# Next batch's query and key steps as single instructions, and 14 weight conversion turns moved to earlier batches

## The chip, the cores and the metric

The kernel runs on one core of a Trainium2 chip. The metric is the time of one execution on the device, in microseconds (us). The engines are named as in the profile: PE (TensorE, matrix products), DVE (VectorE), ACT (ScalarE), POOL (GpSimd), SP (SyncE, which issues all transfers here). Each works through its own instructions in its own order and waits on semaphores for the others.

## The reference

```
# attention over 8 batches, 8 heads, 576 positions, head size 64
q_s = exp(q - max over a head of q);  q_s /= sum over the head + 1e-9
k_s = exp(k - max over positions);    k_s /= sum over positions + 1e-9
x   = q_s @ (k_s^T @ v)                        # 576 x 512 per batch
# gated MLP
h = gelu_tanh(x @ w_in);  u, v = halves of h
v_n = layer_norm(v) * g_ln
x   = x + (u * (w_sg @ v_n + b_sg)) @ w_out
# mixing over positions and over channels
u = x + (x^T @ U @ V)^T
out = u + relu(u @ w_ch1) @ w_ch2              # 512 -> 2048 -> 512
```

## The kernel before

Every product is made of three PE passes over operands split in a high part (`xh`, rounded) and a low part (`xl`, the rest). So behind most results ACT copies the high part, and DVE or POOL subtracts it to get the low part.

Eight batches run one after the other, numbered 0 to 7, each in the same stages. The V stage (`emit_Vh`, five row tiles t = 0 to 4) gives the v half of h in `pv`; ACT applies the gelu to give `ge`, DVE takes mean and variance (`stats`), and `emit_ln` normalizes. The V stage also transposes the batch before (`emit_yT`, tiles `pt`, `yh`, `yl`) and does its small mixing product (`pp`, `pst`, `pw`, `yt`), which goes to DRAM as `u2d`. The U stage (`emit_Uh`, four blocks f) gives the u half in `pu`, whose gelu is `ut`. The S stage (`emit_S`) mixes positions in `pS`, and DVE makes `gt`, `gl` from it. The y stage multiplies by w_out in `py` and adds x to give `yt`; the next batch's attention products stand around it. After batch 7 comes the long product with w_ch1 and w_ch2 (tile `mm`, recursive in the manner of Strassen, over stored weight combinations `wd` that are read back as `wu`), which PE does from about 632 us to the end.

During the stages of batch b the queries and keys of batch b + 1 are made ready on DVE, ACT and POOL, in five row tiles of 128 rows (the last holds 64 queries): `q_max` (tile `qm`), `q_sub`, `q_exp`, `q_sum` (tile `qs`), `q_total`, `q_norm`, `k_sub` and `k_exp`. The queries come into one tile `qt`, loaded by `load_q` in two transfers (rows of tiles 0 to 3, line 133, and the last 64 rows, line 134) during the y stage of the batch before.

The weights w_ch1 and w_ch2 arrive as float64 pairs of words and are converted piece by piece beside the batches. A turn (`turn`, a 'T' in the table `TURNS`) moves this by a step: load `stg` (SP), clamp it (L171, mostly POOL), shift its exponent (L177, ACT), merge the words (L183 and L184, DVE), add blocks to factors (`f<-f,f`, POOL or DVE), copy the high part to `chw` (ACT), subtract it (POOL or DVE), and store to `wd` (SP). `TURNS[b]` gives the turns after each V tile, U block, S block, y block; `STEP_TURNS` and `GROUP_TURNS` go on from there after batch 7, until all weights are done. In batch 7 the first tiles of the channel product (`us`, `uh`, `ul`) are made as well, by `u_first` and `u_parts`.

The order on PE is by hand. The order on DVE is the order of the code (`in_order(dve)`); on ACT, POOL and SP a scheduler sets it in the batches. An instruction that waits holds back what is behind it on its engine. On SP a transfer whose source isn't ready holds back the loads behind it.

Of the kernel before, what the change touches and what calls it, by code (L numbers as in the profile page):

```python
# [22 lines left out]
def fused_kernel(tc, q, k, v, w_in, g_ln, w_sgT, b_sg, w_out, U, V, w_ch1, w_ch2, outT):  # L23
# [412 lines left out]
    def k_exp(b, tiles=range(NT + 1)):
        kt = k_t[b]
        for t in tiles:
            act.activation(kt[:, t], kt[:, t], AF.Exp)
# [13 lines left out]
    def q_sub(b, t, eng=dve):
        n = TR[t]
        tt(eng, q3(t), q3(t), q_s[b][0:n, t].unsqueeze(2).to_broadcast([n, H, D]), ALU.subtract)

    def q_exp(b, t):
        act.activation(qt[0 : TR[t], t], qt[0 : TR[t], t], AF.Exp)

    def q_sum(b, t):  # L460
        if t == 0:
            q_s[b] = tmpp.tile([P, NT + 1, H], F32, tag="qs", name="qs")
        s = q_s[b]
        dve.tensor_reduce(out=s[0 : TR[t], t], in_=q3(t), op=ALU.add, axis=mybir.AxisListType.X)

    def q_total(b):

        s = q_s[b]
        for part in (s[:, 0:NT], s[0:R, NT]):
            dve.tensor_scalar(out=part, in0=part, scalar1=1e-9, scalar2=None, op0=ALU.add)  # L470
            dve.reciprocal(out=part, in_=part)
# [728 lines left out]
    with in_order(dve, act, pool, sp):  # L1200
# [13 lines left out]
        for t in (0, 1):  # L1214
            q_max(0, t)
            q_sub(0, t, dve if t in (3,) else pool)
            q_exp(0, t)
# [4 lines left out]
        k_spread(0)
        for t in range(NT + 1):
            k_sub(0, t)
            k_exp(0, (t,))
            if 0 < t < NT:
                q_exp(0, t + 1)
# [6 lines left out]
        q_total(0)
        for t in range(NT + 1):
            q_norm(0, t, dve)
            if t == 1:
# [16 lines left out]
    for b in range(B):  # L1254
# [52 lines left out]
        late_k = []  # L1307
        for f in range(NF):
# [8 lines left out]
            if f == 0:  # L1317
                emit_ln(b, NT)
                if nxt:
                    load_v(nxt)  # L1320
                else:
                    next(prep, None)
            if nxt:
                for t in Q_SUB[b > 0][f]:
                    q_sub(nxt, t, pool if t in Q_SUB_POOL[b > 0] else dve)
                for t in K_SUB[b > 0][f]:
                    if f >= spread_at:
                        k_sub(nxt, t)
                    else:
                        late_k.append(t)  # L1330
                if f == spread_at:
                    for t in late_k:
                        k_sub(nxt, t)
            if b > 0:
                slot(TURNS[b][1][f])
        if nxt:
            with contextlib.nullcontext() if b else tc.issue_after(last['g', 3].ins):
# [4 lines left out]
            for t in range(NT + 1):  # L1342
                q_sum(nxt, t)
            q_total(nxt)
            for t in range(NT + 1):
                q_norm(nxt, t, dve if t < Q_NORM_DVE[b > 0] else pool)
# [170 lines left out]
```

## Time and profile before

| what | value |
|---|---|
| median of 3 runs | 1308.29 us (1307.48 to 1314.53) |
| the profiled execution | 1311.05 us, span in the trace 1309.2 us |
| PE | busy 1260.0 us, 96% |
| weight loads of PE | busy 1139.1 us, 87% |
| DVE | busy 969.0 us, 74% |
| ACT | busy 636.9 us, 49% |
| POOL | busy 330.4 us, 25% |
| mean granted PE clock | 0.991 of full speed |

Times in the rows count from the start of the span. PE has 49 us of the span without work, and it runs at a lower clock for some stretches; the batches take the first 632 us.

### The profile page before, as it was taken

How to read it: one execution, taken by the hardware profiler on the slowest of the kernel's cores; microseconds unless marked ns; L12 is line 12 of the kernel's file. 1: busy time of each engine (PE TensorE's matmuls, PEld its weight loads, DVE VectorE, ACT ScalarE, POOL GpSimd, SP SyncE). 2: the span in 40 equal slices, each digit the busy share in tenths (PEclk: the TensorE clock that was granted, in tenths of full speed). 3: DMA queues.
4: the chain of work that ended last, by engine and by line, in shares of the span. 5: the costliest groups of instructions: out<-in, count | busy, mean ns of one | idle time of the engine just before them, and what ended most of it. 6: DMA issues, size and time to landing. Idle time of an engine off the chain costs nothing.

```text
span 1309.2 us, 20581 instructions
## 1 busy us (share of the span) xinstructions
PE 1260.0 (96%) x7592; PEld 1139.1 (87%) x7592; DVE 969.0 (74%) x1406; ACT 636.9 (49%) x979; POOL 330.4 (25%) x426
## 2 busy tenths in 40 slices
PE   4799999999999999898999999999999999999998
PEld 3598999999898989798888888888888889999998
DVE  7888879787988888788668953598337963694485
ACT  4756656575757466654454512444134422451342
POOL 4634152624243333665340202000010002000000
PEclk9899999999999999998999999999999999999999
DMA  8515171725343352468998667678756788899896
GB/s 268 164 47 171 37 218 37 225 70 167 96 151 120 111 168 73 162 208 299 312 344 315 227 231 257 209 242 290 257 193 226 243 285 297 269 304 315 260 290 215
DMA packets 135907, 274.14 MB, mean 209 GB/s; under 512 B 15232, under 2 KB 56704, under 8 KB 135808
## 3 DMA queue, kind: packets, MB, share of 16 engines
q1 hardware_dynamic: 135808, 272.84, 63.2%
q8 instruction: 60, 0.98, 0.3%
q14 instruction: 39, 0.32, 0.1%
HBM read 224.56 MB, written 48.23 MB: 208 GB/s over the span
## 4 chain that ended last, share of the span: by engine, by line
PE 79%; DVE 7%; DMA 4%; ACT 2%; issue 1%; POOL 1%; SPq 0%; DVEq 0%; ACTq 0%; POOLq 0%
PE mm L52 50%; PE pS L52 6%; PE pu L52 6%; PE pv L52 5%; PE py L52 5%; DMA stg<-in_w_ch_dram 1%; PE pm L52 1%; PE pp L52 1%; PE px L52 1%; PE pt L698 1%; DVE yt L55 1%; DVE f L183 1%; PE pk L52 1%; PE pt L527 1%; DMA wu<-wd 1%
## 5 line engine op out<-in xcount | busy, mean ns | idle before, releaser
L52 PE MATMUL mm<-oh,wu 128*128 128x512 f32 (+1 forms) x1120 | 320.7, 367 | 0.0
L52 PE MATMUL mm<-uh,wu 128*128 128x512 f32 (+1 forms) x1064 | 303.7, 366 | 1.9 <-DMA wu<-wd 1.1
L52 PEld LDWEIGHTS mm<-oh,wu 128*128 128x128 f32 x1120 | 207.0, 188 | 26.1
L52 PEld LDWEIGHTS mm<-uh,wu 128*128 128x128 f32 x1064 | 196.3, 188 | 26.4 <-issue 1.4
L52 PE MATMUL mm<-ol,wu 128*128 128x512 f32 (+1 forms) x560 | 205.7, 367 | 0.0
L61 ACT ACTIVATE oh<-h 128x1024 fp32r<-128x1024 f32 (+1 forms) x140 | 135.2, 973 | 124.8 <-PE mm L52 102.4
L52 PE MATMUL mm<-ul,wu 128*128 128x512 f32 (+1 forms) x532 | 194.9, 366 | 0.0
L55 DVE TENSOR_TENSOR ol<-h,oh 128x1024 fp32r<-128x1024 f32 (+1 forms) x140 | 155.4, 1113 | 40.9 <-ACT oh L61 40.1
L55 POOL TENSOR_TENSOR ust<-ust 128x1024 f32<-128x1024 f32 (+1 forms) x16 | 36.4, 2282 | 389.4 <-DMA ust<-u2d 348.8
L55 DVE TENSOR_TENSOR h<-mm,u 128x1024 f32<-128x1024 f32 (+1 forms) x57 | 63.3, 1111 | 87.8 <-PE mm L52 87.7
L52 PEld LDWEIGHTS mm<-ol,wu 128*128 128x128 f32 x560 | 105.2, 188 | 13.1
L55 DVE TENSOR_TENSOR u<-mm,u 128x1024 f32<-128x1024 f32 (+1 forms) x53 | 58.9, 1111 | 76.7 <-PE mm L52 71.3
L52 PEld LDWEIGHTS mm<-ul,wu 128*128 128x128 f32 x532 | 99.9, 188 | 12.1
L55 POOL TENSOR_TENSOR chw<-f,chw 128x256 fp32r<-128x256 f32 x98 | 78.9, 820 | 95.4 <-ACT chw L61 95.3
L55 DVE TENSOR_TENSOR h<-h,h 128x1024 f32<-128x1024 f32 (+1 forms) x80 | 88.9, 1112 | 0.0
L1041 ACT ACTIVATE h<-mm 128x1024 f32<-128x1024 f32 (+1 forms) x19 | 17.8, 938 | 130.8 <-PE mm L52 130.8
L1032 ACT ACTIVATE h<-h 128x1024 f32<-128x1024 f32 (+1 forms) x60 | 58.1, 969 | 33.9 <-DVE h L55 33.9
L61 ACT ACTIVATE chw<-f 128x256 fp32r<-128x256 f32 x112 | 42.6, 412 | 62.7 <-DVE f L184 23.1
L61 ACT ACTIVATE u<-mm 128x1024 f32<-128x1024 f32 (+1 forms) x24 | 22.5, 939 | 103.1 <-PE mm L52 86.9
L171 POOL TENSOR_SCALAR stg<-stg 128x256 f32<-128x256 f32 (+1 forms) x83 | 41.0, 496 | 99.7 <-DMA stg<-in_w_ch_dram 39.0
L52 PE MATMUL py<-gh,wo_h 128*128 128x288 f32 x256 | 57.6, 307 | 3.0 <-DVE gt L665 2.1
L52 PE MATMUL py<-gl,wo_h 128*128 128x288 f32 x256 | 56.0, 301 | 3.4 <-DVE gl L55 3.4
(165 smaller groups left out, 2650.2 us busy)
## 6 DMA issues: line engine op xcount, KB each, us to landing
wu<-wd SPq DMA_DIRECT2D x280, 512.0 KB, 4.4
wd<-chw SPq DMA_DIRECT2D x112, 256.0 KB, 3.6
stg<-in_w_ch_dram SPq DMA_DIRECT2D x64, 256.0 KB, 3.7
u2d<-yt SPq DMA_DIRECT2D x32, 288.0 KB, 2.4
vt<-in_v_dram SPq DMA_DIRECT2D x32, 256.0 KB, 6.7
qt<-in_q_dram SPq DMA_DIRECT2D x7, 1024.0 KB, 8.1
kt<-in_k_dram SPq DMA_DIRECT2D x7, 1024.0 KB, 6.1
res<-u2d SPq DMA_DIRECT2D x12, 512.0 KB, 5.3
```

The costliest lines, as they stand in the source:

```text
L52: pe.matmul(out, lhsT, rhs, start=first, stop=last, skip_group_check=onto)
L55: return eng.tensor_tensor(out=out, in0=a, in1=b, op=op)
L61: return act.activation(out, src, AF.Copy)
L171: eng.tensor_scalar(out=hi, in0=hi, scalar1=F64_MOST, scalar2=-F64_MOST, op0=ALU.min, op1=ALU.max)
L183: dve.tensor_scalar(out=b, in0=b, scalar1=3, scalar2=None, op0=ALU.logical_shift_left)
L527: pe.transpose(pt[:, t * P : (t + 1) * P], qt[:, t, c * P : (c + 1) * P], ident)
L698: pe.transpose(pt[0:n, c * P : (c + 1) * P], y_t[b][:, c, t * P : t * P + n], ident)
L1032: act.activation(h, h, AF.Relu)
L1041: act.activation(h_out(j, 11, n), bank, AF.Relu)
```

## The change

The query and key steps of the next batch become one instruction each over all five tiles, where there were five: `q_max`, `q_sub`, `k_sub`, `q_exp`, `k_exp`, `q_sum`, and `q_norm` (in two pieces for the batch after batch 0); `q_total` treats the whole tile in one pair of instructions. The whole `q_max` stands at V tile 0 (at tile 1 in batch 0), the whole `q_sub` at U block 1, the whole `k_sub` at U block 3. The first batch's own preparation stays in tiles. `emit_ln` of the last tile moves from behind U block 0 to behind block 1. The small instruction that makes `sh` becomes a tensor_scalar with two scalars in place of a scalar_tensor_tensor with two tensors. Two of the buffers of `u_parts` change places. `TURNS` of batches 2 to 5 gains 3, 4, 4 and 4 turns, that of batch 7 loses 4 in the V stage, 1 in the U stage and 5 in the S stage; 5 fewer are left for the stretch behind the batches.

```diff
-    def k_sub(b, t, eng=dve):
-        kt = k_t[b]
-        tt(eng, kt[:, t], kt[:, t], kx_t[b], ALU.subtract)
+    ALL = slice(0, NT + 1)
+
+    def k_sub(b, ts=ALL):
+        k = k_t[b][:, ts]
+        tt(dve, k, k, kx_t[b].unsqueeze(1).to_broadcast([P, ts.stop - ts.start, C]), ALU.subtract)
...
-    def q_max(b, t):
-        if t == 0:
-            q_s[b] = tmpp.tile([P, NT + 1, H], F32, tag="qm", name="qm")
-        dve.tensor_reduce(
-            out=q_s[b][0 : TR[t], t], in_=q3(t), op=ALU.max, axis=mybir.AxisListType.X
-        )
+    def q_reduce(tag, ts, op):
+        s = q_s[tag]
+        out = s[:, ts].rearrange("p t h -> p (t h)")
+        dve.tensor_reduce(out=out, in_=heads(ts), op=op, axis=mybir.AxisListType.X)
+
+    def q_max(ts=ALL):
+        if ts.start == 0:
+            q_s["qm"] = tmpp.tile([P, NT + 1, H], F32, tag="qm", name="qm")
+        q_reduce("qm", ts, ALU.max)
...
+    def q_exp(ts=ALL):
+        act.activation(qt[:, ts], qt[:, ts], AF.Exp)
...
-        dve.scalar_tensor_tensor(
-            out=shift[0:n], in0=mv[0:n, 0:1], scalar=-1.0, in1=mv[0:n, 1:2], op0=ALU.mult, op1=ALU.mult
+        dve.tensor_scalar(
+            out=shift[0:n], in0=mv[0:n, 0:1], scalar1=mv[0:n, 1:2], scalar2=-1.0, op0=ALU.mult, op1=ALU.mult
         )
...
-        (('TTT', 'TT', 'TT', 'TTT', 'TT'), ('TT', 'T', 'T', 'TTT'), ('TT', 'T', 'TTTT', 'T'), ('TTT', 'TTT', 'TPTT', 'TT')),
+        (('TT', 'T', 'T', 'TT', 'TT'), ('TT', 'T', 'T', 'TT'), ('T', 'T', '', 'T'), ('TTT', 'TTT', 'TPTT', 'TT')),
...
-    Q_MAX = (((0, 1), (2, 3), (), (4,), ()), ((0, 1, 2), (3,), (4,), (), ()))
+    Q_MAX_AT = (1, 0)
...
-                    for t2 in Q_MAX[b > 0][t]:
-                        q_max(nxt, t2)
+                    if t == Q_MAX_AT[b > 0]:
+                        q_max()
...
-                for t in range(NT + 1):
-                    q_exp(nxt, t)
+                q_exp()
```

How the order on the engines changes is seen at three places. The first is DVE in the V stage of batch 3 (batches 1, 2, 4, 5 and 6 read alike). Before:

```order
L449 TENSOR_REDUCE qm<-qt 128x8 x3
L55 TENSOR_TENSOR yl_3081<-pt_3075,yh_3080 128x512
L610 BN_STATS bst<-ge 128x6
L611 BN_AGGR mv<-bst 128x2
L612 TENSOR_SCALAR mv<-mv 128x1
L55 TENSOR_TENSOR yl_3121<-pt_3115,yh_3120 128x512
L449 TENSOR_REDUCE qm<-qt 128x8
L610 BN_STATS bst<-ge 128x6
L611 BN_AGGR mv<-bst 128x2
L612 TENSOR_SCALAR mv<-mv 128x1
L620 SCALAR_TENSOR_TENSOR sh<-mv 128x1
L55 TENSOR_TENSOR yl_3159<-pt_3153,yh_3158 128x512
L55 TENSOR_TENSOR yh_3167<-pt_3162,yh_3167 64x512
```

And with the change:

```order
L454 TENSOR_REDUCE qm<-qt 128x40
L55 TENSOR_TENSOR yl_3008<-pt_3002,yh_3007 128x512
L614 BN_STATS bst<-ge 128x6
L615 BN_AGGR mv<-bst 128x2
L616 TENSOR_SCALAR mv<-mv 128x1
L55 TENSOR_TENSOR yl_3046<-pt_3040,yh_3045 128x512
L614 BN_STATS bst<-ge 128x6
L615 BN_AGGR mv<-bst 128x2
L616 TENSOR_SCALAR mv<-mv 128x1
L624 TENSOR_SCALAR sh<-mv 128x1
```

All five query tiles now stand ahead of the first `yl` of these rows, where three did; the two `qm` further down are gone.

The second place is DVE at the end of the S stage of batch 7, from the second `gt` pair to the last `gl`. Before:

```order
L55 TENSOR_TENSOR ul_6824<-us,uh_6823 128x512
L55 TENSOR_TENSOR ul_6822<-us,uh_6821 128x512
L55 TENSOR_TENSOR gl_6982<-gt,gh 128x576
L55 TENSOR_TENSOR f_6963<-f_6924,f_6963 128x256
L665 SCALAR_TENSOR_TENSOR gt<-pS,gl,bb 128x576
L55 TENSOR_TENSOR ul_6827<-us,uh_6826 128x512
L55 TENSOR_TENSOR ul_7096<-us_6833,uh_6825 128x512
L55 TENSOR_TENSOR gl_6982<-gt,gh 128x576
L55 TENSOR_TENSOR f_6924<-f_6849,f_6924 128x256
L665 SCALAR_TENSOR_TENSOR gt<-pS,gl,bb 128x576
L55 TENSOR_TENSOR gt<-gt,ut 128x576
L55 TENSOR_TENSOR gl_6982<-gt,gh 128x576 x2
```

With the change:

```order
L55 TENSOR_TENSOR ul_6667<-us,uh_6666 128x512
L55 TENSOR_TENSOR ul_6665<-us,uh_6664 128x512
L55 TENSOR_TENSOR gl_6827<-gt,gh 128x576
L669 SCALAR_TENSOR_TENSOR gt<-pS,gl,bb 128x576
L55 TENSOR_TENSOR ul_6670<-us_6675,uh_6669 128x512
L55 TENSOR_TENSOR ul_6939<-us,uh_6668 128x512
L55 TENSOR_TENSOR gl_6827<-gt,gh 128x576
L669 SCALAR_TENSOR_TENSOR gt<-pS,gl,bb 128x576
L55 TENSOR_TENSOR gt<-gt,ut 128x576
L55 TENSOR_TENSOR gl_6827<-gt,gh 128x576 x2
```

Two factor additions (`f<-f,f`) have left this stretch.

The third place is SP in batch 4, where the queries of batch 6 are loaded (`qt`). Before:

```order
L384 DMA wd_2_6_76<-chw 128x512
L384 DMA wd_2_7_77<-chw 128x512
L384 DMA wd_2_3_80<-chw 128x512
L213 DMA stg<-in_w_ch_dram 128x512 x2
L133 DMA qt<-in_q_dram 128x4x512
L134 DMA qt<-in_q_dram 64x512
L213 DMA stg<-in_w_ch_dram 128x512
L384 DMA wd_2_4_79<-chw 128x512
L147 DMA vt<-in_v_dram 64x4x128
L125 DMA kt<-in_k_dram 128x4x512
```

With the change:

```order
L213 DMA stg<-in_w_ch_dram 128x512
L384 DMA wd_2_6_76<-chw 128x512
L133 DMA qt<-in_q_dram 128x4x512
L384 DMA wd_2_7_77<-chw 128x512
L134 DMA qt<-in_q_dram 64x512
L384 DMA wd_2_3_80<-chw 128x512
L213 DMA stg<-in_w_ch_dram 128x512 x3
L384 DMA wd_3_4_86<-chw 128x512
L147 DMA vt<-in_v_dram 64x4x128
L125 DMA kt<-in_k_dram 128x4x512
```

A store of `wd` now stands between the two query transfers.

## Rows read from the trace of the kernel before

**Rows 1.** The profile page, part 1: busy time by engine.
```profile
PE 1260.0 (96%) x7592; PEld 1139.1 (87%) x7592; DVE 969.0 (74%) x1406; ACT 636.9 (49%) x979; POOL 330.4 (25%) x426
```

**Rows 2.** Windows (length, busy PE, PEld, DVE, ACT, POOL, PEclk): batches 3, 7.
```profile
254.50:323.50 69.00, 68.65 (x530) 64.45 (x530) 58.45 (x110) 42.79 (x75) 23.59 (x38) 1.00 0.40 130
534.90:570.10 35.20, 32.32 (x180) 28.15 (x181) 24.33 (x47) 22.93 (x49) 23.43 (x33) 0.95 0.55 183
570.10:590.60 20.50, 17.11 (x128) 16.63 (x126) 20.02 (x28) 10.15 (x21) 12.29 (x14) 0.98 0.54 180
```

**Rows 3.** Timeline of DVE, V stage of batch 3: start, length, operation.
```profile
256.65 1.86 DVE L449 TENSOR_REDUCE qm<-qt 128x8 f32<-128x512 f32 x3
...
260.04 0.68 DVE L55 TENSOR_TENSOR yl<-pt,yh 128x512 fp32r<-128x512 f32 x1
```

**Rows 4.** Timeline of PE, V stages of batches 3 and 2, third tile.
```profile
261.27 0.48 PE L52 MATMUL pv<-wih,xh 128*128 128x512 f32 x1
...
192.17 0.50 PE L52 MATMUL pv<-wih,xh 128*128 128x512 f32 x1 [0.48 <-DVE yl L55]
```

**Rows 5.** Timeline of DVE, V stage of batch 2.
```profile
188.04 1.87 DVE L449 TENSOR_REDUCE qm<-qt 128x8 f32<-128x512 f32 x3 [1.46 <-DMA qt<-in_q_dram]
```

**Rows 6.** Tile qt, stretch 300 to 400 us.
```profile
L133 SPq DMA_DIRECT2D qt<-in_q_dram x2: 379/460/541, 317.6 to 385.3; - x2
...
DMA to landing us min/median/max: 8.0/8.2/8.2
```

**Rows 7.** Groups by form on DVE, 36 to 632 us.
```profile
L183 DVE TENSOR_SCALAR f<-f 128x256 uint32<-128x256 uint32 x73 | 33.8, 462 | 0.1
...
L612 DVE TENSOR_SCALAR mv<-mv 128x1 f32<-128x1 f32 x32 | 4.9, 153 | 1.1
...
L55 DVE TENSOR_TENSOR h<-pm,u 128x1024 f32<-128x1024 f32 x3 | 3.7, 1224 | 2.3 <-PE pm L52 2.3
```

**Rows 8.** Line L620 over the whole trace: shortest, median, longest.
```profile
L620 DVE SCALAR_TENSOR_TENSOR sh<-mv x40: 138/152/2741, 52.3 to 559.6; 128x1 f32<-128x1 f32 x32, 64x1 f32<-64x1 f32 x8
```

**Rows 9.** Timeline of DVE, V stage of batch 7.
```profile
547.37 1.39 DVE L183 TENSOR_SCALAR f<-f 128x256 uint32<-128x256 uint32 x1
...
552.57 1.23 DVE L620 SCALAR_TENSOR_TENSOR sh<-mv 128x1 f32<-128x1 f32 x1
```

**Rows 10.** Timeline of POOL, the same stretch.
```profile
547.13 1.48 POOL L55 TENSOR_TENSOR vl<-ge,vh 128x512 fp32r<-128x512 f32 x1
...
552.33 1.46 POOL L55 TENSOR_TENSOR vl<-ge,vh 128x512 fp32r<-128x512 f32 x1
```

**Rows 11.** Timeline of PE, batch 7: its waits in V and y stages.
```profile
550.07 0.80 PE L52 MATMUL pw<-v_w,pst 128*128 128x288 f32 x4 [0.78 <-DVE pst L55]
...
554.64 1.29 PE L52 MATMUL pw<-v_w,pst 128*128 128x288 f32 x4 [1.84 <-DVE yt L55]
...
590.59 0.85 PE L52 MATMUL py<-gl,wo_h 128*128 128x288 f32 x2 [2.93 <-DVE gl L55]
```

**Rows 12.** Windows around those waits: PEclk is the granted clock.
```profile
556.00:560.00 4.00, 3.96 (x20) 3.96 (x21) 2.69 (x7) 3.10 (x6) 3.54 (x5) 0.62 0.69 246
592.00:596.00 4.00, 4.00 (x18) 4.00 (x18) 3.90 (x9) 0.68 (x2) 1.27 (x1) 0.50 0.93 308
```

**Rows 13.** Timeline of DVE, end of the S stage of batch 7.
```profile
581.26 0.41 DVE L55 TENSOR_TENSOR f<-f,f 128x256 f32<-128x256 f32 x1
...
582.33 3.00 DVE L55 TENSOR_TENSOR ul<-us,uh 128x512 fp32r<-128x512 f32 x2
...
586.46 0.95 DVE L55 TENSOR_TENSOR f<-f,f 128x256 f32<-128x256 f32 x1
...
589.26 1.95 DVE L55 TENSOR_TENSOR gl<-gt,gh 128x576 fp32r<-128x576 f32 x2
```

**Rows 14.** Timeline of POOL, the same stretch.
```profile
582.90 1.87 POOL L55 TENSOR_TENSOR gt<-gt,ut 128x576 f32<-128x576 f32 x1
```

**Rows 15.** Timeline of PE, start of the S stage of batch 6.
```profile
502.70 0.53 PE L52 MATMUL pS<-sg_h,vh 128*128 128x288 f32 x2 [0.84 <-ACT ut L645]
```

More of the change, by code (lines that the diff above doesn't have):

```diff
@@ L430, in k_spread @@
         kx_t[b] = pb.rearrange("p c e -> p (c e)")
-    def k_sub(b, t, eng=dve):
-        kt = k_t[b]
-        tt(eng, kt[:, t], kt[:, t], kx_t[b], ALU.subtract)
[L436 to L439, printed above, removed]
-    q_s = {}
-    def q3(t):
-        return qt[0 : TR[t], t].rearrange("p (h d) -> p h d", d=D)
-    def q_max(b, t):
-        if t == 0:
-            q_s[b] = tmpp.tile([P, NT + 1, H], F32, tag="qm", name="qm")
-        dve.tensor_reduce(
-            out=q_s[b][0 : TR[t], t], in_=q3(t), op=ALU.max, axis=mybir.AxisListType.X
-        )
@@ L453, in q_sub @@
[L453 to L471, printed above, removed]
@@ L473, in q_norm, with k_exp, heads @@
-    def q_norm(b, t, eng=pool):
-        n = TR[t]
-        tt(eng, q3(t), q3(t), q_s[b][0:n, t].unsqueeze(2).to_broadcast([n, H, D]), ALU.mult)
+    ALL = slice(0, NT + 1)
+    def k_sub(b, ts=ALL):
+        k = k_t[b][:, ts]
+        tt(dve, k, k, kx_t[b].unsqueeze(1).to_broadcast([P, ts.stop - ts.start, C]), ALU.subtract)
+    def k_exp(b, ts=ALL):
+        k = k_t[b][:, ts]
+        act.activation(k, k, AF.Exp)
+    q_s = {}
+    def heads(ts):
+        return qt[:, ts].rearrange("p t (h d) -> p (t h) d", d=D)
@@ new lines, in per_head @@
+    def per_head(s, ts):
+        n = (ts.stop - ts.start) * H
+        return s[:, ts].rearrange("p t h -> p (t h)").unsqueeze(2).to_broadcast([P, n, D])
+    def q_reduce(tag, ts, op):
[6 more added lines that the diff above has]
+        q_reduce("qm", ts, ALU.max)
@@ new lines, in q_sub, with q_sum, q_total @@
+    def q_sub(ts=ALL, eng=dve):
+        tt(eng, heads(ts), heads(ts), per_head(q_s["qm"], ts), ALU.subtract)
+    def q_exp(ts=ALL):
+        act.activation(qt[:, ts], qt[:, ts], AF.Exp)
+    def q_sum(ts=ALL):
+        if ts.start == 0:
+            q_s["qs"] = tmpp.tile([P, NT + 1, H], F32, tag="qs", name="qs")
+        q_reduce("qs", ts, ALU.add)
+    def q_total():
+        s = q_s["qs"]
+        dve.tensor_scalar(out=s, in0=s, scalar1=1e-9, scalar2=None, op0=ALU.add)
+        dve.reciprocal(out=s, in_=s)
@@ L477, in fused_kernel, with q_norm @@
+    def q_norm(ts=ALL, eng=dve):
+        tt(eng, heads(ts), heads(ts), per_head(q_s["qs"], ts), ALU.mult)
     kv_t = {}
@@ L777, in u_parts @@
         if kc == 0:
-            parts = [tmpp.tile([P, F], F32, tag="ge", name="us", bufs=3) for _ in range(3)]
-            parts.append(wrk.tile([P, F], F32, tag="xr", name="us3"))
+            parts = [tmpp.tile([P, F], F32, tag="ge", name="us", bufs=3) for _ in range(2)]
+            parts.append(wrk.tile([P, F], F32, tag="xr", name="us2"))
+            parts.append(tmpp.tile([P, F], F32, tag="ge", name="us", bufs=3))
         else:
@@ L1187, in fused_kernel @@
     OP = (2, 1, 1, 2, 0, 2, 2, 1, 1)
-    Q_MAX = (((0, 1), (2, 3), (), (4,), ()), ((0, 1, 2), (3,), (4,), (), ()))
+    Q_MAX_AT = (1, 0)
     FOLDS = ((0, 1, 2, 1, 0), (0, 0, 2, 2, 0))
-    Q_SUB = (((0, 1), (2, 3, 4), (), ()),) * 2
-    Q_SUB_POOL = ((3,), ())
-    K_SUB = (((), (), (0, 1, 2), (3, 4)), ((), (), (0,), (1, 2, 3, 4)))
+    Q_SUB_AT = 1
+    K_SUB_AT = 3
     Q_NORM_DVE = (2, 5)
@@ L1213, in fused_kernel @@
         run(k_fold(0))
[L1214 to L1217, printed above, removed]
+        tiles = [slice(t, t + 1) for t in range(NT + 1)]
+        for ts in tiles[0:2]:
+            q_max(ts)
+            q_sub(ts, pool)
+            q_exp(ts)
         k_max(0)
-        for t in range(2, NT + 1):
-            q_max(0, t)
-            q_sub(0, t, dve if t in (3,) else pool)
+        for ts in tiles[2:]:
+            q_max(ts)
+            q_sub(ts, dve if ts.start == 3 else pool)
         k_spread(0)
-        for t in range(NT + 1):
[L1224 to L1227, printed above, removed]
+        for ts in tiles:
+            k_sub(0, ts)
+            k_exp(0, ts)
+            if 0 < ts.start < NT:
+                q_exp(tiles[ts.start + 1])
         more(OP[0])
         emit_kv(0)
-        for t in range(NT + 1):
-            q_sum(0, t)
-            if t == 2:
+        for ts in tiles:
+            q_sum(ts)
+            if ts.start == 2:
                 more(OP[1])
[L1234 to L1237, printed above, removed]
+        q_total()
+        for ts in tiles:
+            q_norm(ts)
+            if ts.start == 1:
                 more(OP[2])
@@ L1306, in fused_kernel @@
             prep = u_first()
-        late_k = []
         for f in range(NF):
@@ L1317, in fused_kernel @@
             if f == 0:
-                emit_ln(b, NT)
                 if nxt:
@@ L1322, in fused_kernel @@
                     next(prep, None)
+            if f == 1:
+                emit_ln(b, NT)
             if nxt:
[L1324 to L1333, printed above, removed]
+                if f == Q_SUB_AT:
+                    q_sub()
+                if f == K_SUB_AT:
+                    k_sub(nxt)
             if b > 0:
@@ L1337, in fused_kernel @@
             with contextlib.nullcontext() if b else tc.issue_after(last['g', 3].ins):
-                for t in range(NT + 1):
-                    q_exp(nxt, t)
+                q_exp()
             with contextlib.nullcontext() if b else tc.issue_after(last['g', 3].ins):
                 k_exp(nxt)
[L1342 to L1346, printed above, removed]
+            q_sum()
+            q_total()
+            split = Q_NORM_DVE[b > 0]
+            q_norm(slice(0, split))
+            if split < NT + 1:
+                q_norm(slice(split, NT + 1), pool)
         if not nxt:
```

8 rows, old and new, of the table TURNS are left out of this document.

## Prediction

> **What bounds the kernel now.** I read the profile page first, then the windows by batch, then the waits of PE and the timelines of the engines that it waits for. The page shows PE busy for 96% of the span [rows 1]: the kernel is bound by PE, and no more can be gained than PE's idle time and what it loses at a low clock. The windows say where that is. In batch 3, which stands for batches 1 to 5, PE works 68.65 of 69.00 us; there is nothing to win there, and anything that delays PE is a plain loss. In batch 7 it is otherwise: the V and U stages hold 35.20 - 32.32 = 2.88 us of idle PE, the S stage 20.50 - 17.11 = 3.39 us, and in the S stage DVE is busy for 20.02 of the 20.50 us [rows 2]. The waits name what ends last there. In the V stage PE waits 0.78 us for `pst` and 1.84 us for `yt`, at the end of the S stage 2.93 us for `gl` [rows 11], all three made by DVE. Behind the second and the third wait the granted clock is low: 0.62 between 556 and 560, 0.50 between 592 and 596, which is the 1.2 GHz level [rows 12]. So a wait of 2 or 3 us there costs more than itself.
>
> **Query maximum, batches 1 to 6.** This is the edit that speaks against the change. In the V stage PE can't begin the product of the third tile before DVE has made the second `yl` of that stretch, which frees its PSUM tile. In batch 3 that `yl` ends at 260.04 + 0.68 = 260.72, and the product starts at 261.27 [rows 3, 4]: 0.55 us to spare. Ahead of it stand three query maxima that take 1.86 us together; with the change all five tiles stand there as one instruction over 2560 elements. The trace has no such instruction. Bounds: five times a third of 1.86 us gives 3.10 us; a DVE instruction over 1024 elements takes 1.22 us [rows 7] and one over 512 takes 0.68 [rows 3], so 0.54 for each further 512, and 0.68 + 4 x 0.54 = 2.84 us. I take 2.85: `yl` comes 1.0 us later, 0.55 are spare, PE stalls 0.45. Batch 2 has no room: there the maximum already waits 1.46 us for the queries, and PE waits 0.48 for `yl` [rows 4, 5], so the 1.0 us counts in full. With batches 1 and 4 to 6 taken like batch 3 the sum is 5 x 0.45 + 1.0 = +3.2 us. Bounds: 0, if something else in the order gives the time back, and 6 x 1.0 = +6.
>
> **The other merged steps.** Each merged DVE step takes 2.84 us by the slope above against 5 x 0.62 = 3.10, so it saves some 0.25 us; they lie in the U stage, where DVE has room (58.45 of 69.00 us busy in a batch [rows 2]), and are hidden behind PE: 0. The cover is thin only where ACT alternates exponentials with `ut`. In batch 6 the S stage starts 0.84 us late for the last `ut` [rows 15], behind two runs of five exponentials. One instruction instead of five pays its start once; I take half of the wait, between 0 and the whole 0.84: -0.4. The batch after batch 0 gets the same edits in stages that are not full; I take 0, bounds +1 and -1, by the 1.0 us that the maximum moves.
>
> **V stage of batch 7.** There is no next batch here, so no query maximum, and only the turns and `sh` change. Ahead of `pst` DVE merges words of two blocks; one of these instructions takes 1.39 us while POOL runs a `vl` of 1.48 us [rows 9, 10], and the two start and end within a quarter of a microsecond of each other. With the change one pair of merges less stands there, and none ahead of the next `sh`. The first instruction of a pair takes 0.46 us in the mean [rows 7]; I take the second for as much or a little less, and a pair for 0.8. The 0.78 us wait should go, and 0.8 of the 1.84. The rest of that wait is `sh`: it took 1.23 us at 552.57 and ended as POOL's `vl` of 1.46 us did [rows 9, 10], while the median of this line is 0.15 and its longest 2.74 [rows 8]. As tensor_scalar with scalars it has one tensor to read; the nearest row is the tensor_scalar of the same size on `mv`, 0.15 us in the mean of 32 [rows 7], which is never drawn out. That gives 1.08 back. So 0.78 + 0.8 + 1.04 = 2.6 us of idle PE go, and with the second wait the half clock behind it: 4.0 us at 0.62 is 4.0 x 0.38 = 1.5 us lost [rows 12]. Sum -4.1, bounds 0 (other merges slide into the same places) and -4.4.
>
> The Trainium skill bears on `sh` (SBUF — State Buffer, "Who interferes with whom"): a DVE instruction with two SBUF tensors shares a port with GpSimd and whoever starts first holds it to the end, and tensor_scalar can enter a two-port mode that contends just as well. The drawn-out merge of 1.39 us is a tensor_scalar, and the one on `mv` never is, so this trace shows both sides of that rule. If the new form contended too, 1.08 us would stay, and the sum below would be -3.7 instead of -4.8.
>
> **S and y stages of batch 7.** DVE is the chain here. Out of it go two factor additions of 0.41 and 0.95 us [rows 13]. The count of merges up to the last `gt` stays at four pairs in this stage, one of them later. Further, two `ul` take 3.00 us, where a subtraction of that size takes 0.68 [rows 3], and two `gl` 1.95 [rows 13], where 0.68 for 512 elements makes 0.76 for their 576 and 1.5 for two; POOL is at `gt` for 1.87 us just then [rows 14], and additions follow. With 5 fewer turns POOL has less to do there; `gt` stays on POOL, so I count half of the 1.6 + 0.5 us: 1.1. Together 0.41 + 0.95 + 1.1 = 2.5 of the 3.39 us of idle PE. What stays is a wait of about 0.9 us, and a wait of that size left the clock alone at `pS` in batch 6 [rows 15]; so the low clock goes too. Behind the 2.93 us wait it costs 4.0 x 0.50 = 2.0 us from 592 to 596 alone [rows 12]; I count 2.5 with the edges. Sum -5.0, bounds 0 (the stall stays long enough to lower the clock) and -6.5.
>
> **The turns in batches 2 to 5.** Fifteen turns more on engines with room: DVE 58 of 69 us, ACT 43, POOL 24 [rows 2]. By themselves they cost nothing, since PE waits for none of it. What they touch is SP: in batch 4 a store of `wd` comes between the two query transfers, and one query maximum now needs both. The load issued at 385.3 lands 8.2 us after its issue [rows 6], so about 393.5 for the first and some tenths later for the second, and the maximum of the next V stage begins with hardly any time to spare, as the wait of 1.46 us in batch 2 shows [rows 5]. If the store waits for its `chw`, queries, maximum, `yl` and PE are late by as much. I take +1.5, bounds 0 and +5.
>
> **Sum.** +3.2 - 0.4 - 4.1 - 5.0 + 1.5 = -4.8 us. Against the profiled execution, 1311.05 us, that is 1306.2; against the median of 1308.29 us it is 1303.5, which is the forecast, since the 2.8 us between the two are spread that the change doesn't touch.
>
> **Rivals.**
> *All of batch 7's loss goes and the V stages don't pay.* The waits of batch 7 vanish with their low clock (-4.4 - 6.5), the longer maximum hides: -10.9 - 0.4, about 1297. For it: DVE is the only engine that PE waits for there. Against it: the 0.55 us of room in batch 3 are less than the shift.
> *Only the V stage of batch 7 gains.* DVE stays full in the S stage, because the stretch comes from POOL's `gt`, which stays, and the low clock stays with it: +3.2 - 0.4 - 4.1 + 1.5 = +0.2, about 1308.5. For it: DVE 20.02 of 20.50 us busy.
> *Slower: the queries come late.* The one maximum stands at the head of DVE's order in the V stage, and `yl` behind it. If it waits 2 us or more for its second transfer in four of the five full batches, PE loses 8 us, with the +3.2 of the V stages more than batch 7 gives: -4.8 - 1.5 + 12 = +5.7 or more, 1314 to 1318. It decides from a delay of about 2 us a batch. Against it: the order shows a store between the transfers in one batch only.
>
> **How the numbers follow.** A measurement tells 0.5% from no change, 6.5 us: below 1301.8 is faster, above 1314.8 slower. Chances: the forecast 0.42 (1300 to 1307), all gained 0.20, V stage only 0.29, slower 0.09. Faster is the second case with something over four tenths of the first: 0.20 + 0.18 = 0.38. Slower 0.09, the same 0.53. The range leaves out the tail of each side: 1295.5 to 1313.
>
> **What would show it.** Right: in V stages of batches 1 to 6 a `qm` of 2.8 us and a PE wait of 0.3 to 1.0 us for `yl` at the third tile; in batch 7 no wait of over 1 us for `yt`, the clock at 1.00 from 556 on, the wait for `gl` under 1 us and no 0.50 between 592 and 596; `sh` at 0.15 us. Wrong, if PE waits for nothing in those V stages (then `yl` has more room than I read), if the clock still falls at the end of the S stage (then POOL holds DVE there whatever the turns do), or if `qm` waits for its transfer in more than one batch.

## The result and the profile after

The changed kernel takes 1320.7 us (median of 6 runs, 1317.97 to 1321.59) against 1308.55 us: ratio 1.0081, 95% interval [1.0067, 1.0095]. It is slower by 12.2 us between the medians, by 10.6 us as the ratio has it; the forecast was 1303.5 us, with a range of 1295.5 to 1313. Its profiled execution took 1318.06 us, with a span of 1316.3 us. PE's busy time, part 1 of the page, is that of before; DVE, ACT and POOL have less to do:

```profile
PE 1260.5 (96%) x7592; PEld 1135.4 (86%) x7592; DVE 959.4 (73%) x1256; ACT 627.6 (48%) x921; POOL 319.9 (24%) x421
```

So the span got longer by idle time of PE. (It is 7 us longer between the two profiled executions, of which the one before lies above its median and the one after below; 1 us of that lies in the first 37 us, and other runs here vary there by as much.) The waits of PE up to the long product, in us in total, times, longest:

```profile
PE py L52 <- DVE yt L55: 6.0, 5, 1.7
...
PE pv L52 <- DVE xl L55: 2.5, 7, 0.6
PE pv L52 <- ACT ge L604: 2.2, 7, 0.9
...
PE py L52 <- DVE gl L55: 1.3, 1, 1.3
PE pu L52 <- DVE ge L55: 1.3, 1, 1.3
```

The largest new wait is that of `py` for `yt`, a tile of the y stage, where the kernel before lost almost nothing. These are the windows of S and y stage of batch 3, before (length, busy PE, PEld, DVE, ACT, POOL, clock):

```profile
286.80:305.40 18.60, 18.60 (x205) 18.36 (x203) 16.87 (x32) 10.12 (x18) 1.94 (x2) 1.00 0.16 52
305.40:323.45 18.05, 18.05 (x142) 17.90 (x139) 12.68 (x24) 9.95 (x22) 10.76 (x19) 1.00 0.60 201
```

and after, with the V and U stages and the S stage of batch 7 behind them, and two windows around its waits:

```profile
291.20:309.80 18.60, 18.60 (x204) 18.36 (x203) 18.32 (x21) 11.54 (x15) 6.55 (x8) 1.00 0.19 66
309.80:329.80 20.00, 18.31 (x141) 17.93 (x139) 15.04 (x29) 9.75 (x23) 13.32 (x22) 1.00 0.67 217
546.50:581.70 35.20, 32.84 (x187) 29.03 (x186) 23.71 (x50) 22.89 (x46) 17.94 (x26) 0.95 0.49 161
581.70:602.20 20.50, 19.07 (x141) 18.47 (x140) 18.47 (x29) 7.69 (x15) 5.95 (x8) 1.00 0.62 206
566.00:570.00 4.00, 3.90 (x19) 3.91 (x20) 2.35 (x7) 2.79 (x5) 2.89 (x4) 0.62 0.96 326
600.00:604.00 4.00, 3.92 (x29) 3.92 (x30) 3.94 (x7) 1.36 (x3) 1.84 (x2) 1.00 0.99 379
```

In batch 3 the y stage grew from 18.05 to 20.00 us, and PE stood still for 1.69 of them; DVE has 2.4 us more to do there and POOL 2.6 us more. In the S stage ahead of it DVE is full (18.32 of 18.60 us, from 16.87), yet PE loses nothing there. In batch 7 the window of the S stage [rows 2] has 1.43 us of idle PE instead of 3.39, and no low clock from 600 on, where the kernel before had 0.50 behind its wait for `gl` [rows 12]. The V stage still ends in a wait, and the clock is still at 0.62 behind it.

Where the time went, by the first matrix product of each stage in PE's timeline (from the first `py` of a batch to the first `pv` of the next; the last line from batch 7's first `pv` to the first `mm`), in us:

| stage | before | after | y turns undone | y turns only | factors on POOL |
|---|---|---|---|---|---|
| y of batch 2 | 18.05 | 20.16 | 19.83 | 18.35 | 18.11 |
| y of batch 3 | 18.05 | 20.01 | 18.05 | 18.09 | 19.04 |
| y of batch 4 | 18.06 | 19.51 | 18.09 | 21.90 | 18.18 |
| y of batch 5 | 18.22 | 19.68 | 18.05 | 18.05 | 18.37 |
| y of batch 6 | 19.33 | 20.62 | 19.23 | 19.97 | 19.28 |
| batch 7 | 98.71 | 93.32 | 93.15 | 99.05 | 92.63 |

(The last three columns belong to experiments below.) The five y stages lost 8.3 us, the V stages of batches 3, 4 and 6 another 3.5 (20.48, 20.47 and 20.07 us, from 19.15, 19.15 and 19.18), and batch 7 gained 5.4. The longest waits of those V stages are for `xl` (0.57 and 0.42 us in batches 3 and 4) and for `yt` (0.92 in batch 6).

One of the y stages shows how. DVE in batch 3, from `kv` to the first `yt`:

```profile
313.76 0.86 DVE L55 TENSOR_TENSOR kv<-pk,rs 64x256 f32<-64x256 f32 x2
314.65 0.43 DVE L55 TENSOR_TENSOR chw<-f,chw 128x256 fp32r<-128x256 f32 x1
314.99 0.29 DVE L183 TENSOR_SCALAR f<-f 128x256 uint32<-128x256 uint32 x1
315.31 0.42 DVE L184 SCALAR_TENSOR_TENSOR f<-stg,f 128x256 uint32<-128x256 uint32 x1
315.66 1.51 DVE L55 TENSOR_TENSOR chw<-f,chw 128x256 fp32r<-128x256 f32 x1
317.09 0.28 DVE L183 TENSOR_SCALAR f<-f 128x256 uint32<-128x256 uint32 x1
317.40 0.43 DVE L184 SCALAR_TENSOR_TENSOR f<-stg,f 128x256 uint32<-128x256 uint32 x1
317.86 0.76 DVE L55 TENSOR_TENSOR yt<-py,x 128x576 f32<-128x576 f32 x1
```

POOL at that time, and PE:

```profile
315.36 1.52 POOL L55 TENSOR_TENSOR kl<-kv,kh 128x512 fp32r<-128x512 f32 x1 [2.13 <-ACT kh L61]
```

```profile
316.27 0.71 PE L531 MATMUL pt<-ident,qt 128*128 128x128 f32 x5
318.67 0.53 PE L52 MATMUL py<-gh,wo_h 128*128 128x288 f32 x2 [1.69 <-DVE yt L55]
```

Between `kv` and `yt` stand two low parts (`chw`) and two pairs of merges, 3.2 us of conversion. One `chw` takes 1.51 us instead of 0.43: it starts behind POOL's `kl` and ends 0.3 us behind it. PE has finished the second product and its transposes by about 317, and must wait for `yt` to read `py` and free it.

### The profile page after: what moved, and what is told of

It is laid out like the page before. It is cut to its first block, busy times and chain, and to the rows that moved or that the text cites. A ratio compares the mean times of both kernels' runs of the same rounds, so it can differ in the third digit from the quotient of the medians.

```text
span 1316.3 us, 20377 instructions
## 1 busy us (share of the span) xinstructions
PE 1260.5 (96%) x7592; PEld 1135.4 (86%) x7592; DVE 959.4 (73%) x1256; ACT 627.6 (48%) x921; POOL 319.9 (24%) x421
## 4 chain that ended last, share of the span: by engine, by line
PE 58%; DVE 3%; DMA 1%; issue 1%; ACT 1%; POOL 1%; SPq 0%; DVEq 0%; POOLq 0%; ACTq 0%
PE mm L52 50%; PE pu L52 2%; PE pS L52 2%; PE pv L52 1%; PE py L52 1%; DMA wu<-wd 1%; PE pm L52 1%; DVE ul L55 0%; DVE yt L55 0%; DVE f L184 0%; POOL chw L55 0%; DMA stg<-in_w_ch_dram 0%; DMA us<-u2d 0%; PE px L52 0%; DVE f L183 0%
## 5 line engine op out<-in xcount | busy, mean ns | idle before, releaser
L55 POOL TENSOR_TENSOR chw<-f,chw 128x256 fp32r<-128x256 f32 x94 | 76.0, 820 | 72.6 <-ACT chw L61 63.0
L52 PE MATMUL pu<-xh,wih 128*128 128x288 f32 x256 | 57.8, 308 | 1.3 <-DVE ge L55 1.3
```

The costliest lines, as they stand in the source:

```text
L52: pe.matmul(out, lhsT, rhs, start=first, stop=last, skip_group_check=onto)
L55: return eng.tensor_tensor(out=out, in0=a, in1=b, op=op)
```

## The experiments

Two theories stand first: A, that the added turns put conversion ahead of `yt` on DVE in the y stages; B, that the long instructions of the V stages, the query maximum above all, are the loss. Ratios are to the kernel before, run on the same chip.

The tables of the change add fifteen turns to batches 2 to 5 (3, 4, 4 and 4), one more than the title says.

**Which half of the change.** The first run has the changed kernel with the old table `TURNS`, the second the kernel before with the new one.

> The changed kernel with the old table of turns: only the single instructions, sh and the order of emit_ln are new. Theory A (the added turns in batches 2 to 5 put conversion work on DVE ahead of yt in the y stage, and PE waits there): the waits for yt in the y stages go, 6 us or more come back, and batch 7 is as slow as before: about 1309 to 1314 us. Theory B (the long query maximum and the other long instructions in the V stages are the loss): the time stays at 1318 us or more, since batch 7's gain goes as well.

> The kernel before with the new table of turns only. Theory A: slower than before by the yt waits of five batches (6 to 8 us) less the 5 us of batch 7, so 1309 to 1314 us, with waits for yt in the y stages of batches 2 to 6. Theory B: batch 7's gain alone, about 1303 us.

Measured: old turns 1.0047 [1.0030, 1.0064], 1315.39 us; new turns alone 1.0087 [1.0069, 1.0104], 1319.69 us. Both halves are slower by themselves. The new turns alone make a loss as large as the whole, and their y stages show it (20.45, 20.12, 19.22, 19.80, 20.03 us in batches 2 to 6). With the old turns the y stages of batches 2 to 6 are 18.05 to 18.49 again; what that run loses up to batch 7 lies in the V stages (20.04, 20.02 and 19.72 us in batches 3, 5 and 6, from 19.15). In batch 7 `py` to `pm` takes 22.44 us instead of 19.35, which neither theory had, and the rest of the batch makes it up (98.66 us against 98.71).

**Query maximum and sh.** In the changed kernel, the maximum in three pieces as before, and then the old form of `sh`:

```diff
-                    if t == Q_MAX_AT[b > 0]:
-                        q_max()
+                    for lo, hi in Q_MAX[b > 0][t]:
+                        q_max(slice(lo, hi))
```

```diff
-        dve.tensor_scalar(out=shift[0:n], in0=mv[0:n, 0:1], scalar1=mv[0:n, 1:2], scalar2=-1.0, ...)
+        dve.scalar_tensor_tensor(out=shift[0:n], in0=mv[0:n, 0:1], scalar=-1.0, in1=mv[0:n, 1:2], ...)
```

> The changed kernel with the query maximum in the three pieces and at the three places of before. Theory A: it changes the V stages by less than 0.3 us each, so within 2 us of the changed kernel (1316 to 1321). Theory B: 0.5 to 1 us in each of six V stages and more behind them, so 1311 to 1315 us.

> The changed kernel with the old two-tensor form of sh. If the form matters only where PE waits for what stands behind it (V stages, some tenths of a us in each, and batch 7), 1 to 4 us slower than the changed kernel, with sh drawn out to over 1 us in places; if DVE's order hides it, no change.

Measured: 1.0075 [1.0056, 1.0095] and 1.0080 [1.0059, 1.0101]; neither can be told from the changed kernel. The old `sh` is still drawn out in places (shortest, median, longest in ns), the new one never, but is 0.05 us longer each time. The old form:

```profile
L624 DVE SCALAR_TENSOR_TENSOR sh<-mv x40: 138/154/1273, 54.6 to 576.3; 128x1 f32<-128x1 f32 x32, 64x1 f32<-64x1 f32 x8
```

The new form in the changed kernel:

```profile
L624 DVE TENSOR_SCALAR sh<-mv x40: 195/203/210, 54.8 to 572.9; 128x1 f32<-128x1 f32 x32, 64x1 f32<-64x1 f32 x8
```

The V stage of batch 7 takes 20.94 us with the old form and 20.92 with the new. That is no test of the 1.23 us of the kernel before [rows 9], since the old form takes 0.36, 0.15 and 0.26 us there until just before the stage's end: the long one didn't come back. What the run shows is that a drawn-out `sh` elsewhere costs nothing that can be told.

**Batch 7's turns against those of batches 2 to 5.** On the kernel before: the ten turns out of batch 7 alone, done in the first steps behind the batches; and the fifteen added turns alone.

```diff
-    GROUP_TURNS = (1, 1, 2, 2, 2, 2, 2, 2, 2, 2, 3, 3, 2, 3, 4, 1, 0, 1, 3, 3)
+    GROUP_TURNS = (2, 2, 3, 3, 3, 3, 3, 2, 2, 2, 3, 3, 3, 3, 4, 1, 1, 2, 3, 3)
...
-        (('TTT', 'TT', 'TT', 'TTT', 'TT'), ('TT', 'T', 'T', 'TTT'), ('TT', 'T', 'TTTT', 'T'), ('TTT', 'TTT', 'TPTT', 'TT')),
+        (('TT', 'T', 'T', 'TT', 'TT'), ('TT', 'T', 'T', 'TT'), ('T', 'T', '', 'T'), ('TTT', 'TTT', 'TPTT', 'TT')),
```

> The kernel before with the ten turns taken out of batch 7 alone and done in the first steps behind the batches (GROUP_TURNS raised by ten in all). If the relief of batch 7 is real by itself: the wait for gl under 1.5 us instead of 2.9, batch 7 shorter by 4 to 6 us, 1302 to 1305 us in all, unless the ten turns make weight combinations late behind the batches, which would show as PE waits for wu at some 640 to 700 us. If batch 7's gain came from somewhere else in the change: 1308 us.

> The kernel before with the fifteen added turns of batches 2 to 5 alone, batch 7 as before. Theory A: the whole loss of the turns without batch 7's gain, the 10.8 us of the table plus 4 to 6 us: 1321 to 1326 us, waits for yt in the y stages of batches 2 to 6. If the added turns cost little and the table's loss lies in batch 7 or behind it: about 1309 us.

Measured: batch 7 relieved alone 1.0021 [1.0012, 1.0030]; the fifteen turns alone 1.0138 [1.0117, 1.0160], some 18 us. From the second to the run with the whole table the ratio falls by 0.0051, 6.7 us give or take 3.6: that is what batch 7's relief is worth with the work done earlier. By itself its long product starts at 629.4 us instead of 632.0 and then gives 5.1 us back, of which 3.5 are waits for late weights and for `u` (waits of PE from there on):

```profile
PE mm L52 <- DMA wu<-wd: 3.4, 3, 1.8
PE mm L52 <- ACT u L61: 1.2, 1, 1.2
```

These were 1.1 us for `wu` and none for `u` in the kernel before.

**The later emit_ln.** The last tile's `emit_ln` back behind U block 0, in the changed kernel and in the one with the old turns:

```diff
             if f == 0:
+                emit_ln(b, NT)
...
-            if f == 1:
-                emit_ln(b, NT)
```

> The changed kernel with the last tile's emit_ln back behind U block 0. If the later emit_ln holds DVE in the U stage of batch 7 (3.5 us idle for vh in the run with the old turns), the first ul and us come earlier and 0 to 3 us come back: 1317 to 1320 us; in the other batches nothing.

> The merged steps and the new sh with the old turns, and the last tile's emit_ln back behind U block 0. If the loss of that run (6.5 us) lies in batch 7 behind the later emit_ln: the two waits for gl (3.5 and 2.2 us) fall to the 2.9 us of before, and 1309 to 1311 us. If it lies in the merged steps: 1314 to 1316 us.

Measured: 1.0057 [1.0041, 1.0073] and 1.0016 [1.0006, 1.0025], against 1.0081 and 1.0047. With the old turns the gain is clear, 0.3% or 4 us, of which 2.7 us show in batch 7 (95.94 us from `pv` to `mm`, from 98.66). With the new turns the intervals overlap. In the run with old turns and the later `emit_ln`, DVE in the U stage of batch 7 reads

```profile
570.48 0.69 DVE L55 TENSOR_TENSOR vh<-ge,vh 64x512 fp32r<-64x512 f32 x1 [3.55 <-ACT vh L61]
571.20 0.69 DVE L55 TENSOR_TENSOR ul<-us,uh 128x512 fp32r<-128x512 f32 x1
574.06 0.69 DVE L55 TENSOR_TENSOR us<-us 128x512 f32<-128x512 f32 x1 [2.17 <-issue]
```

DVE waits 3.55 us for ACT's `vh` of the last tile, and the first parts of the channel product, which don't need it, stand behind. PE pays at the end of the S stage:

```profile
591.19 0.85 PE L52 MATMUL py<-gl,wo_h 128*128 128x288 f32 x2 [3.54 <-DVE gl L55]
...
595.18 0.85 PE L52 MATMUL py<-gl,wo_h 128*128 128x288 f32 x2 [2.18 <-DVE gl L55]
```

With the early one that `us` starts 4.3 us sooner (3.8 counted from the batch's first `pv`), and the two waits are 0.57 and 2.92 us instead of 3.54 and 2.18:

```profile
569.80 0.69 DVE L55 TENSOR_TENSOR us<-us 128x512 f32<-128x512 f32 x1 [2.07 <-POOL chw L55]
```

**Place or number of the turns.** From the changed kernel, the eight turns added in y stages taken out again; and the six added in U stages taken out instead. The rows of batch 3, of the changed kernel and then of each run:

```diff
-        (('', '', '', '', 'T'), ('T', '', 'T', 'T'), ('', 'TT', 'TTT', 'TTT'), ('TT', 'TTT', 'TT', 'T'), ...
+        (('', '', '', '', 'T'), ('T', '', 'T', 'T'), ('', 'TT', 'TTT', 'TTT'), ('TT', 'TTT', 'T', ''), ...
...
+        (('', '', '', '', 'T'), ('T', '', '', ''), ('', 'TT', 'TTT', 'TTT'), ('TT', 'TTT', 'TT', 'T'), ...
```

> The changed kernel without the eight turns added in the y stages of batches 2 to 5; the six added in U stages and the one in an S stage stay. Theory A1 (a turn added in the y stage puts its own conversion ahead of yt there): the y stages of batches 2 to 5 fall from 19.5 to 20.2 us to near 18.1, 6 to 8 us come back, 1310 to 1313 us. Theory A2 (turns added in the U stage fill DVE in the S stage, and what is left over runs into the y stage): the y stages stay at 19.5 us or more in batches 2 to 4, and 1316 us or more.

> The changed kernel without the six turns added in the U stages of batches 2 to 4; those of the y and S stages stay. Theory A1: the y stages stay at 19.5 us or more, 1316 us or more. Theory A2: the S stage of batch 3 has DVE busy for 17 us instead of 18.3, the y stages of batches 2 to 4 fall towards 18.1, and 5 to 8 us come back.

Measured: without the y turns 1.0000 [0.9986, 1.0013], without the U turns 1.0098 [1.0074, 1.0121]. Taking the eight turns of the y stages out gives the whole loss back; taking the six out gives nothing back that can be told. On the kernel before the turns outside the y stages do cost something: 6 us, give or take 3.5, by the fifteen together (1.0138) against the eight alone (1.0090, below). In the profile 2.5 of them are waits of PE for `gt` at the end of the S stage of batch 2, which no kernel with the merged steps has. The S stage of batch 3 is as full without the y turns as in the changed kernel (DVE 18.29 of 18.60 us), so a full DVE there isn't the cause. Theory B, as the main loss, has fallen with the split maximum. Neither A1 nor A2 holds as it was put: without the y turns the y stage of batch 2 stays at 19.83 us, and without the U turns those of batches 2 and 3 fall to 18.92 and 18.88, while that of batch 4 grows to 21.79. Without the y turns, DVE ahead of the first `yt` of batch 3 is:

```profile
313.38 0.86 DVE L55 TENSOR_TENSOR kv<-pk,rs 64x256 f32<-64x256 f32 x2
314.26 0.43 DVE L55 TENSOR_TENSOR chw<-f,chw 128x256 fp32r<-128x256 f32 x1
314.61 0.29 DVE L183 TENSOR_SCALAR f<-f 128x256 uint32<-128x256 uint32 x1
314.93 0.43 DVE L184 SCALAR_TENSOR_TENSOR f<-stg,f 128x256 uint32<-128x256 uint32 x1
315.38 0.76 DVE L55 TENSOR_TENSOR yt<-py,x 128x576 f32<-128x576 f32 x1
```

one `chw` and one pair instead of two of each; `yt` starts at 315.38 and PE doesn't wait. Three further runs ask what in those eight turns it is: the eight moved to the U stages of the same batches; the eight alone on the kernel before; the changed kernel with the tables `DVE_FACTOR_LOWS` and `DVE_FACTOR_SUMS` empty, which puts the factor additions and low parts of batches 2 to 6 on POOL.

> The changed kernel with the eight turns added in y stages placed in the U stages of the same batches, so the number of turns by batch stays. Place: the y stages are near 18.1 us, and 1309 to 1313 us. Number: the work comes out in the y stages all the same, 1316 us or more.

> The kernel before with only the eight turns added in the y stages of batches 2 to 5, batch 7 as before. Place: y stages of some 19.5 to 20 us in batches 2 to 6 and 8 to 14 us more than before, 1317 to 1324 us. If the turns cost only together with those of the U stages: within 3 us of before.

> The changed kernel with all factor additions and low parts of batches 2 to 6 on POOL (in the changed kernel up to two and five a batch are on DVE). If what delays yt is those steps on DVE: y stages back near 18.1 us and 1310 to 1314 us. If POOL then becomes late itself, or holds DVE's two-tensor instructions more often: 1318 us or more.

Measured: 1.0038 [1.0021, 1.0055]; 1.0090 [1.0074, 1.0106]; 1.0026 [1.0012, 1.0040]. Moved to the U stages the same number of turns costs half; with the factor steps off DVE the full table costs a third. Place and number are not told apart by these runs, since each changes a third thing too: which steps fall where. A turn does the next steps of a cycle of eleven (four blocks to merge, seven factors to make), so one turn more moves the steps of all later slots. In batches 2, 3 and 4 the slot ahead of the first `yt` has three, two and three turns in both tables; the added ones stand behind it. What it holds differs all the same. The traces give the conversion on DVE between `kv` and the first `yt` (a pair is the two instructions of a merge), the end of that `yt` counted from the stage's first `py`, and PE's wait for it, in us:

| run | batch 2 | batch 3 | batch 4 |
|---|---|---|---|
| before | none, 4.52, 0 | 1 addition, 5.86, 0 | 1 low part, 4.70, 0 |
| after | 2 pairs and 1 low part, 8.31, 1.19 | 2 pairs and 2 low parts, 8.82, 1.69 | 2 low parts and 1 addition, 7.95, 0.83 |
| y turns undone | 2 pairs and 1 low part, 8.18, 1.06 | 1 pair and 1 low part, 6.42, 0 | 2 pairs, 6.44, 0 |
| U turns undone | none, 5.43, 0 | none, 6.69, 0 | 2 pairs and 1 low part, 9.94, 1.86 |
| y turns only | none, 4.51, 0 | none, 5.89, 0 | 2 pairs and 1 low part, 9.84, 1.77 |

Where this `yt` ends within 6.7 us PE doesn't wait for it, and where it ends at 7.9 us or later PE does. In batch 3 the run with the y turns alone, whose row has both added turns, has no conversion there:

```profile
314.21 0.86 DVE L55 TENSOR_TENSOR kv<-pk,rs 64x256 f32<-64x256 f32 x2
315.10 0.76 DVE L55 TENSOR_TENSOR yt<-py,x 128x576 f32<-128x576 f32 x1
```

So the cause is DVE's conversion ahead of the first `yt`, and in these batches the added turns bring it there by shifting the cycle, not by standing there. With the factors on POOL the low parts are gone from DVE, though the merges take up to 1.40 us beside a busier POOL:

```profile
313.36 0.86 DVE L55 TENSOR_TENSOR kv<-pk,rs 64x256 f32<-64x256 f32 x2
314.25 0.70 DVE L183 TENSOR_SCALAR f<-f 128x256 uint32<-128x256 uint32 x1
314.98 0.85 DVE L184 SCALAR_TENSOR_TENSOR f<-stg,f 128x256 uint32<-128x256 uint32 x1
315.75 0.83 DVE L183 TENSOR_SCALAR f<-f 128x256 uint32<-128x256 uint32 x1
316.62 1.40 DVE L184 SCALAR_TENSOR_TENSOR f<-stg,f 128x256 uint32<-128x256 uint32 x1
318.05 0.76 DVE L55 TENSOR_TENSOR yt<-py,x 128x576 f32<-128x576 f32 x1
```

`yt` starts 4.69 us after `kv`, where it took 4.10 in the changed kernel; but `kv` starts sooner there, and PE waits 0.72 us in place of 1.69. The y stage of batch 3 takes 19.04 us, those of batches 2, 4, 5 and 6 take 18.11 to 19.28. The y turns alone lose at other places in the profiled run: 1.8 us for `yt` in batch 4, and also two query maxima that wait for their transfer, 3.2 us in batch 2 and this one in batch 4:

```profile
333.04 1.87 DVE L449 TENSOR_REDUCE qm<-qt 128x8 f32<-128x512 f32 x3 [2.92 <-DMA qt<-in_q_dram]
```

**Versions.** The merged steps with old turns, early `emit_ln` and the maximum in three pieces; the same with five turns of batch 7's S stage moved behind the batches; and the changed kernel without the y turns, with early `emit_ln` and the split maximum.

> Merged steps and new sh, old turns, early emit_ln, and the query maximum in the three pieces of before. If the one long maximum costs some 0.3 us in each V stage of batches 1 to 6, 1 to 2 us less than with it (ratio 1.0016): a ratio of 1.000 to 1.001. If it costs nothing: 1.0016 again.

> As the run beside it, with the five turns of batch 7's S stage moved behind the batches (one more in each of the first five steps there). If DVE's work in the S stage is what makes gl late: the wait for gl under 1.5 us and the low clock behind it gone, batch 7 shorter by 4 to 5 us; behind the batches the run with ten turns moved lost some 5 us to late wu, with five it should be 0 to 2.5: a ratio of 0.997 to 1.000.

> The changed kernel without the eight turns of the y stages (ratio 1.000 by itself), with the early emit_ln (0.24% less on the changed kernel) and the query maximum in three pieces (0.26% less on the merged steps). If the three add: a ratio of 0.995 to 0.997, 1303 to 1306 us. If they share the same slack: 0.998 to 1.000.

Measured: 0.9990 [0.9976, 1.0004], 0.9972 [0.9961, 0.9984], 0.9959 [0.9945, 0.9974]. The split maximum is worth 0.26% with the old turns. The five turns of the S stage alone bring 0.2%, with intervals that overlap; the wait for `gl` of 2.93 us [rows 11] is 0.96 there. The last version, 1304.72 us, beats the kernel before by 0.41% and the changed one by 1.2%: five of the change's edits kept (merged steps, new `sh`, fewer turns in batch 7, more in U and S stages of batches 2 to 5, and the exchange of two buffers of `u_parts`, which no run tries alone) and three undone.

## Why the prediction was wrong

**The turns in batches 2 to 5 were mis-sized: the step that failed.** The forecast has "By themselves they cost nothing, since PE waits for none of it", and +1.5 us for late queries. The fifteen turns cost some 18 us on the kernel before. In the changed kernel taking out the eight of the y stages gives the whole loss back, and PE waits 5.4 us for the first `yt` of batches 2, 3, 4 and 6, where it waited for none. The step read the room of DVE from a whole batch, 58 of 69 us. But a busy share says nothing of the order: in the y stage `yt` stands behind whatever conversion falls into the slot ahead of it. The rows that would have shown it were these of the kernel before, DVE in batch 3 from `kv` to the first `yt`, and the product of PE that uses its place:

```profile
309.15 0.86 DVE L55 TENSOR_TENSOR kv<-pk,rs 64x256 f32<-64x256 f32 x2
310.04 0.42 DVE L55 TENSOR_TENSOR f<-f,f 128x256 f32<-128x256 f32 x1
310.50 0.76 DVE L55 TENSOR_TENSOR yt<-py,x 128x576 f32<-128x576 f32 x1
```

```profile
312.33 0.50 PE L52 MATMUL py<-gh,wo_h 128*128 128x288 f32 x2
```

One addition stands there; `yt` ends at 311.26 and is needed at 312.33, so there is about 1 us to spare. The changed kernel has two pairs of merges and two low parts in its place, 3.2 us against 0.5. Nor did the prediction ask which steps the longer table would bring where. That table shifts which step falls into every later slot, and so changes what stands ahead of the first `yt` in batches 2, 3 and 4, whose slot there gained no turn, and in batch 6, whose row is unchanged (three pairs, a wait of 1.69 us).

**Batch 7.** The mechanism was right; the sum of -9.1 was nearer to -5.4 in the profiled runs, -6.7 give or take 3.6 by the two ratios. The S and y stages gave 4.5 us (19.35 to 14.88 from `py` to `pm`) of 5.0 forecast: the wait is 1.33 instead of 2.93, the low clock gone. (In the other runs with this row of batch 7 that stretch takes 14.8 to 18.9 us, so how near the size came is partly luck.) The V stage gave 1.9 of 4.1: PE now waits 0.90 and 1.33 us for `ge` in place of `pst` and `yt`, which brings the low clock back at 566 to 570. Whether the 1.08 us for `sh` came isn't shown: the run with the old form takes the same time in this stage, but its `sh` is short there.

**The query maximum.** Its duration was right, 2.81 us, as were those of the other merged steps, while the exponentials took 2.35 us in place of 2.72:

```profile
L55 DVE TENSOR_TENSOR qt<-qt,qm 128x2560 f32<-128x2560 f32 x7 | 19.9, 2838 | 0.2
L454 DVE TENSOR_REDUCE qm<-qt 128x40 f32<-128x2560 f32 x7 | 19.7, 2811 | 0.1
L465 ACT ACTIVATE qt<-qt 128x2560 f32<-128x2560 f32 x7 | 16.4, 2349 | 1.2 <-DVE qt L55 1.1
```

The -0.4 us for the exponentials was of the right kind: the wait for `ut` is gone, and the S stage of batch 6 takes 18.56 us in every kernel with the merged steps, where those with single steps take 18.61 to 19.66. But the price, +3.2 us by a wait for `yl` at the third tile, was wrong. In batch 4 `yl` and the third tile's `pv` are

```profile
333.26 2.81 DVE L454 TENSOR_REDUCE qm<-qt 128x40 f32<-128x2560 f32 x1
335.98 0.68 DVE L55 TENSOR_TENSOR yl<-pt,yh 128x512 fp32r<-128x512 f32 x1
...
337.59 0.68 DVE L55 TENSOR_TENSOR yl<-pt,yh 128x512 fp32r<-128x512 f32 x1
```

```profile
337.82 0.50 PE L52 MATMUL pv<-wih,xh 128*128 128x512 f32 x1
```

`pv` starts before the second `yl` has ended. The traces name the semaphore that this product waits on. In batches 1 to 6 of every kernel with the maximum in pieces it is one that only DVE counts up, in those of every kernel with the maximum whole one that only ACT counts up. So the edit itself took away the wait that was to price it. That fits a PSUM buffer that another engine had freed; which buffer it was isn't shown. With the maximum in three pieces PE does wait for `yl` there when the queries are late (1.36 us in batch 2 of the run with the five turns moved). The V stages of batches 1 and 5 take 0.3 us more (19.44 and 19.42 against 19.14), most of it lost in a wait for `yt` at their ends (0.23 and 0.24 us).

**Not costed at all.** The later `emit_ln` stands among the edits, and the prediction gave it no price. It cost 4 us with the old turns; with the new ones, where the gap is 0.24%, the runs leave it open.

**The late queries.** In the profiled execution no `qm` waits for a transfer, though a store stands between the two. In each of the other runs one does, with the maximum whole or in pieces, for 1.0 to 3.8 us at the longest, and in the kernel before for 1.46 us [rows 5]; the changed kernel with the old `sh`, which has the same turns, shows 3.8. So the wait is real, but it changes from one execution to the next and isn't the loss of the change. That rival had the direction right by another cause.

## What to carry to other kernels

Room on an engine is a property of a place in its order, not of a stage: before background work is added at a slot, read what stands behind that slot and when another engine needs it. A table of slots that drives a pipeline of steps shifts every later step too, so a row that isn't edited changes as well: list what each later slot will hold, before and after. And when several edits come together, price each one, also the one that looks like tidying: here an unpriced one cost 4 us beside the old turns.
